# Attention and feed-forward in one kernel: softmax's end of odd batches in the left-over pass, three banks there, and three smaller moves

## The chip, the cores and the metric

The kernel runs on one core of a Trainium2 chip. The metric is device time in microseconds (us) of one execution, the median of several. The engines spoken of are TensorE (PE in the profile; its weight loads are a row of their own, PEld), VectorE (DVE), ScalarE (ACT) and the queue that starts transfers (SP). They run side by side; each works through its own list of instructions in order, and an instruction waits until what it reads is written and what it overwrites has been read.

## What is computed

Per batch (8) and head (8) the 576 positions are pooled into 32 slots and attended to; then a feed-forward layer with SiLU over all 4608 tokens (512 wide, 2048 inside). The reference, cut:

```python
a = np.exp(phi - np.max(phi, axis=2, keepdims=True))          # phi: batch, head, position, slot
a = a / (np.sum(a, axis=2, keepdims=True) + 1e-09)
k_m = np.einsum('bhsm,bhsd->bhmd', a, k)
v_m = np.einsum('bhsm,bhsd->bhmd', a, v)
scores = scale * np.matmul(q, k_m.transpose(0, 1, 3, 2))
scores = np.exp(scores - np.max(scores, axis=-1, keepdims=True))
attn = scores / (np.sum(scores, axis=-1, keepdims=True) + 1e-09)
x = np.matmul(attn, v_m)                                      # -> tokens x 512
h = x @ w_in
out = (h * (1.0 / (1.0 + np.exp(-h)))) @ w_out
```

## The kernel before

Everything is in 32 bits; a product of two such matrices is made of three matmuls, of high and low parts (hi*hi, hi*lo, lo*hi), so each operand exists as a rounded high part and the remainder, the low part. ScalarE usually makes the high part by a copy, VectorE the low part by a subtraction.

The kernel runs over the eight batches, b = 0 to 7. The attention of batch b+1 is computed in the gaps of batch b's feed-forward. v_m and w_in are multiplied first into one matrix P of the batch (`p_mm`, L631, then `p_split`: ScalarE L647 and VectorE L649), in four blocks of 512 columns; h is then the softmax times P. All blocks go through one tile in PSUM, `bg`, so a block's matmuls wait until VectorE has split the block before.

From batch 2 on the feed-forward goes in 16 steps, called slots (`for s in range(NFC)`, L1210): two halves t of the tokens, eight pairs j of 128-column groups each. A slot issues the h matmuls (`ffn1s`, L822), then `forms` (ScalarE's SiLU L836 and L838 and high parts L840 and L850; VectorE's sums L841 to L845 and low parts L851 and L852, all in the buffer `gbuf` and its splits), then whatever `events` hold for this slot (`run`), then the output products of the slot before (`st_step`, L861). These products are a Strassen-like scheme: four sums in four PSUM banks (tag `acc`, four buffers, given out in turn), 21 matmuls per step, 14 with the high part of the activations (HIGH) and 7 with the low part (LOW). After the last step of a half, `st_out` empties the banks: ScalarE copies banks 0 and 1 (L892), VectorE adds from banks 2 and 3 (L899), and four stores follow.

512 of a batch's 576 tokens go this way. The 64 others wait in `gleft` and are done for two batches together, behind each odd batch, in the left-over pass: four steps (slots 16 to 19) of `left_split` (ScalarE L924, VectorE L925) and `left_st` (24 matmuls, also L861, tiles `lsum`), the last of which is issued in slot 0 of the next batch. In two banks it keeps three sums; after the last step ScalarE copies a part of bank 0 (L945), VectorE adds it to the others (L946, L947), and the rows go out (L950).

What an event does and when is a table, `steady` (L957) for batches 2 to 6 and a list for batches 0 and 1 (L1018): `ev(b, slot, function, batch, ...)`. The names that matter: `s_max`, `s_sub`, `s_exp`, `s_sum` (VectorE L438 to L440) and `s_norm` (L444) are the softmax of the next batch; `s_back` turns it back (two VectorE transposes L459, one ScalarE copy L460 that is the high part) and `s_low` makes the low part (L467). FIRST and SECOND are halves of the tokens. `phi_max` (L258 to L261), `phi_fold` (L286 to L304, over small transfers) and `phi_sub` (L312, L315) prepare the exponential of phi for the batch after that. `exp_slots` (L828) are slots in which ScalarE changes its table for an exponential.

PE's and, from batch 1, ACT's lists keep the order in which the code is written. VectorE's list is laid out by the scheduler, which `behind(...)` ties at some places to the instruction before. In batch 0 events in the slots 11 and later stand behind the last split of SiLU's result; batches 0 and 1 use plain accumulation (`ffn1` L671, `ffn2` L714, `silu` L696 and L698).

## Time and profile before

| | us |
|---|---|
| median of three runs | 692.52 (690.91 to 693.7) |
| the profiled execution | 690.7 |
| its span in the profile | 688.9 |
| VectorE busy | 516.0 (75%) |
| ScalarE busy | 367.1 (53%) |

The span runs from the first to the last instruction of the profiled execution; the 1.8 us beside it are start and end. Rows of the timeline read: start, duration, engine, line, operation, tile written <- tiles read, shape, count; in brackets how long the engine had stood idle just before, and which instruction ended the wait. Several equal instructions are one row. Matmuls overlap: the next begins before the one ahead of it has left the array, so the start of the next row tells more than a row's duration.

### The profile page before, as it was taken

The page shows a single profiled execution, that of the slowest core. Times are in us where ns is not written, and L with a number is a line of the kernel's source. Part 1 is how long each engine was busy: PE and PEld are TensorE (multiplying, and loading weights), DVE is VectorE, ACT ScalarE, POOL GpSimd, SP SyncE. Part 2 cuts the span into 40 slices and gives each one's busy share as a digit, 9 for nine tenths or more (in the row PEclk, how much of TensorE's full clock was granted, in tenths as well). Part 3 has the DMA queues.
Part 4 walks back from the last instruction along what each step waited for, and adds up shares of the span by engine and source line. Part 5 has one row for each costly group of instructions (what it writes and reads, how often), then busy time and mean ns, then how long its engine had stood idle before and what let it go on. Part 6 is the DMA issues. An engine that isn't in the chain of part 4 may idle for free.

```text
span 688.9 us, 14787 instructions
## 1 busy us (share of the span) xinstructions
PE 675.3 (98%) x5932; PEld 596.0 (87%) x5932; DVE 516.0 (75%) x1085; ACT 367.1 (53%) x676; POOL 0.7 (0%) x6
## 2 busy tenths in 40 slices
PE   8899999999999998999999999999999999999997
PEld 3578777787889997899898999899989999889996
DVE  4897899988938588868885588876885668867652
ACT  3878684543535555644645546564653636554441
POOL 0000000000000000000000000000000000000000
PEclk9999999999999999999999999999999999999999
DMA  9988975224360561254420444125430204300001
GB/s 342 352 335 276 326 282 206 90 78 161 104 206 1 175 222 62 78 189 146 139 92 17 165 127 167 69 86 181 153 124 31 79 1 154 110 30 17 31 1 47
DMA packets 37748, 93.93 MB, mean 136 GB/s; under 512 B 4656, under 2 KB 21168, under 8 KB 34096
## 3 DMA queue, kind: packets, MB, share of 16 engines
q1 hardware_dynamic: 36736, 90.22, 38.0%
q10 hardware_dynamic: 944, 2.77, 1.0%
q8 instruction: 47, 0.77, 0.5%
q14 instruction: 21, 0.17, 0.1%
HBM read 77.22 MB, written 15.73 MB: 135 GB/s over the span
## 4 chain that ended last, share of the span: by engine, by line
PE 76%; DVE 6%; ACT 3%; issue 1%; DMA 1%; SPq 0%; DVEq 0%; ACTq 0%
PE sum L861 33%; PE h L822 21%; PE acc L714 5%; PE lsum L861 5%; PE bg L631 3%; PE h L671 3%; PE accleft L714 2%; PE bg L335 1%; PE bg L382 1%; DVE pm L649 1%; DVE gparts L688 1%; DMA fm<-fm 1%; ACT pm L647 0%; DVE aT L459 0%; DVE wf L782 0%
## 5 line engine op out<-in xcount | busy, mean ns | idle before, releaser
L822 PE MATMUL h<-aparts,pm 128*128 128x288 f32 x1152 | 169.1, 296 | 0.0
L822 PEld LDWEIGHTS h<-aparts,pm 128*128 128x128 f32 x1152 | 157.0, 188 | 1.2 <-issue 0.7
L836 ACT ACTIVATE gbuf<-h 128x512 f32<-128x512 f32 x96 | 57.2, 596 | 127.4 <-PE h L822 125.5
L861 PE MATMUL sum<-wo_hi,aparts 128*128 128x256 f32 x384 | 104.2, 293 | 0.7 <-ACT aparts L850 0.7
L841 DVE TENSOR_TENSOR gbuf<-gbuf 128x256 f32<-128x256 f32 x96 | 40.5, 422 | 83.0 <-ACT gbuf L836 82.5
L861 PE MATMUL sum<-kept,aparts 128*128 128x256 f32 x576 | 100.2, 282 | 0.0
L861 PE MATMUL sum<-wo_lo,aparts 128*128 128x256 f32 x384 | 100.0, 282 | 0.0
L861 PEld LDWEIGHTS sum<-wo_hi,aparts 128*128 128x128 f32 x384 | 72.7, 189 | 20.3 <-ACT gleft L838 16.7
L850 ACT ACTIVATE aparts<-gbuf 128x512 fp32r<-128x512 f32 x86 | 54.4, 633 | 65.8 <-DVE gbuf L845 65.8
L714 PE MATMUL acc<-wo_hi,gparts 128*128 128x512 f32 x256 | 85.1, 397 | 0.1
L861 PEld LDWEIGHTS sum<-kept,aparts 128*128 128x128 f32 x576 | 82.5, 191 | 0.0
L852 DVE TENSOR_TENSOR gparts<-gbuf,aparts 128x512 fp32r<-128x512 f32 x86 | 59.4, 691 | 18.6 <-ACT aparts L850 18.6
L861 PEld LDWEIGHTS sum<-wo_lo,aparts 128*128 128x128 f32 x384 | 73.1, 190 | 0.0
L861 PE MATMUL sum<-wo_hi,gparts 128*128 128x256 f32 x384 | 72.7, 281 | 0.0
L861 PE MATMUL sum<-kept,gparts 128*128 128x256 f32 x288 | 65.5, 282 | 0.0
L714 PEld LDWEIGHTS acc<-wo_hi,gparts 128*128 128x128 f32 x256 | 47.5, 188 | 14.0 <-DVE t L804 1.7
L861 PEld LDWEIGHTS sum<-wo_hi,gparts 128*128 128x128 f32 x384 | 59.4, 190 | 0.0
L671 PEld LDWEIGHTS h<-aparts,pm 128*128 128x128 f32 x372 | 51.8, 188 | 7.3 <-issue 2.7
L671 PE MATMUL h<-aparts,pm 128*128 128x288 f32 x372 | 56.1, 299 | 0.8 <-ACT aparts L599 0.4
L840 ACT ACTIVATE aparts<-gbuf 128x384 fp32r<-128x384 f32 x96 | 50.4, 525 | 0.0
L714 PE MATMUL acc<-wo_lo,gparts 128*128 128x512 f32 x128 | 49.4, 393 | 0.4 <-DVE wo_lo L182 0.3
L861 PEld LDWEIGHTS sum<-kept,gparts 128*128 128x128 f32 x288 | 47.9, 190 | 0.0
(204 smaller groups left out, 987.8 us busy)
## 6 DMA issues: line engine op xcount, KB each, us to landing
win<-win_saved SPq DMA_DIRECT2D x24, 1024.0 KB, 4.9
kv<-in_kv SPq DMA_DIRECT2D x28, 516.0 KB, 4.8
q<-in_q SPq DMA_DIRECT2D x16, 576.0 KB, 5.1
raw<-in_w_in SPq DMA_DIRECT2D x14, 512.0 KB, 7.3
raw<-in_w_out SPq DMA_DIRECT2D x6, 1024.0 KB, 6.8
win_saved<-win SPq DMA_DIRECT2D x4, 1024.0 KB, 8.7
phi<-in_phi SPq DMA_DIRECT2D x7, 576.0 KB, 5.9
out<-oo SPq DMA_DIRECT2D x26, 128.0 KB, 1.8
```

Source lines behind the costliest of these rows:

```text
L335: nc.tensor.matmul(pt[p][M * r : M * (r + 1), :KVW], e[:, p, c, M * r : M * (r + 1)], kvt[c][:, p, r], start=c == 0, stop=False, skip_grou ...
L382: nc.tensor.matmul(to[M * r : M * (r + 1)], kvT[D * p : D * (p + 1), 0, r], at[b]["q", hf][D * p : D * (p + 1), r, f : f + n], start=True, ...
L631: nc.tensor.matmul(bg[M * r : M * (r + 1), p, :w].rearrange("p (k f) -> p k f", f=P), kvT[D * p : D * (p + 1), 1, r], src[D * p : D * (p + ...
L671: nc.tensor.matmul(h[:, hf, :HALF], wt[:, p, fs], a[:, p, hf * HALF : (hf + 1) * HALF], start=n[hf] == 0, stop=n[hf] == 5, skip_group_chec ...
L714: nc.tensor.matmul(acc[key], gt[:, cs], wt[:, fc], start=fc == 0 and n == 0, stop=fc == NFC - 1 and n == 2)
L822: nc.tensor.matmul(h[:, i, :HALF], wt[:, p, f : f + P], a[:, p], start=n == 0, stop=n == 5)
L836: nc.scalar.activation(gbuf[:, :MAIN].rearrange("p (i f) -> p i f", i=2), h[:, :, :w], AF.Silu)
L840: nc.scalar.activation(hi[:, :3], g[:, 1:4], AF.Copy)
L841: nc.vector.tensor_tensor(g[:, 4:6], g[:, :1].broadcast_to([P, 2, P]), g[:, 1:3], op=ALU.subtract)
L850: nc.scalar.activation(hi[:, 3:], g[:, 4:], AF.Copy)
L852: last_split.append(nc.vector.tensor_tensor(lo[:, 3:], g[:, 4:], hi[:, 3:], op=ALU.subtract))
L861: nc.tensor.matmul(sums[bank][:, place * Q : (place + 1) * Q], gt[:, k], wt, start=bank not in begun, stop=True, skip_group_check=True,)
```

## The change

Six edits, all in the order of work and in where it lands; nothing is computed differently.

- `s_back` of batches 4 and 6, first half, and its `s_low` move from slot 14 of the batch before to slot 19, the last of the left-over pass. Its landing place there is the first half of `gbuf`, not the tile `cva`.
- `s_back` of batch 1 runs in two halves: four transposes of 288 and two copies.
- In the last step of each half of a batch, `st_step` issues the two LOW products of bank 0 ahead of the HIGH products of bank 2.
- `left_st` uses three banks and goes through them one after the other within a step; in the last step the copy and the first add follow as soon as their bank is done, and each half of the columns is stored on its own.
- In batch 2 `s_sum` moves from slot 12 to slot 11, `s_norm` from 13 to 12, and the second block of P of batch 3 from slot 14 to 15.
- `phi_sub` for batches 5 and 7 moves from slot 17 to slot 1 of the next batch, where it stands for the other batches already; and in batch 0 `phi_max` stands behind the last split.

```diff
@@ -453,11 +453,16 @@
             set_parts(b)
         w = u[1] - u[0]
         tag = "cva" if b > 2 else ("x", "y")[b - 1]
-        aT = at[b]["aT"][u] = sb.tile([P, 2, w], F32, tag=tag, name=f"aT{b}", bufs=1)
-        c = slice(*u)
-        for p in range(2):
-            last_turn[:] = [nc.vector.transpose(aT[:, p], at[b]["sc"][:, p, c])]
-        nc.scalar.activation(at[b]["ahi"][:, :, c], aT, AF.Copy)
+        if b > 2 and b % 2 == 0 and u == FIRST:
+            aT = gbuf[:, : 2 * w].rearrange("p (g s) -> p g s", g=2)
+        else:
+            aT = sb.tile([P, 2, w], F32, tag=tag, name=f"aT{b}", bufs=1)
+        at[b]["aT"][u] = aT
+        for v in (FIRST, SECOND) if b == 1 else (u,):
+            c, to = slice(*v), slice(v[0] - u[0], v[1] - u[0])
+            for p in range(2):
+                last_turn[:] = [nc.vector.transpose(aT[:, p, to], at[b]["sc"][:, p, c])]
+            nc.scalar.activation(at[b]["ahi"][:, :, c], aT[:, :, to], AF.Copy)
 
     def s_low(b, u):
         ahi, alo = (at[b][k] for k in ("ahi", "alo"))
@@ -879,8 +884,11 @@
         todo = (
             (0, 0, 0, b11), (0, 1, 2, b21), (3, 0, 1, t4), (1, 0, 6, b22), (1, 1, 4, b12), (2, 0, 5, t2), (2, 1, 3, t3)
         )
-        for terms in (HIGH, LOW):
-            for bank, place, k, w in todo:
+        order = [(HIGH, todo), (LOW, todo)]
+        if j == NP - 1:
+            order = [(HIGH, todo[:5]), (LOW, todo[:2]), (HIGH, todo[5:]), (LOW, todo[2:])]
+        for terms, some in order:
+            for bank, place, k, w in some:
                 product(bank, place, part, k, w, terms)
         if j == NP - 1:
             st_out(b, t)
@@ -927,27 +935,28 @@
 
     def left_st(b, n, gs):
         if n == 0:
-            sums[:] = [ps.tile([P, DMODEL], F32, tag="acc", name=f"lsum{i}", bufs=NI) for i in range(2)]
+            sums[:] = [ps.tile([P, DMODEL], F32, tag="acc", name=f"lsum{i}", bufs=NI) for i in range(3)]
             begun.clear()
         part = [x.rearrange("p (n f) -> p n f", f=P) for x in gs]
-        for i in range(2):
-            j = 2 * n + i
-            for k in range(2):
-                ws = [
-                    (wo_hi[:, 2 * j + k, q * Q : (q + 1) * Q], wo_lo[:, 2 * j + k, q * Q : (q + 1) * Q])
-                    for q in range(2)
-                ]
-                product(k, 0, part, 2 * i + k, ws[0], HIGH + LOW)
-                product(0, 1, part, 2 * i + k, ws[1], HIGH + LOW)
-        if n == NLS - 1:
+        last = n == NLS - 1
+        if last:
             o = sb.tile([P, DMODEL], F32, tag="cva", name="ol", bufs=1)
             x = sb.tile([P, Q], F32, tag="cva1", name="xl", bufs=1)
-            nc.scalar.activation(x, sums[0][:, :Q], AF.Copy)
-            nc.vector.tensor_tensor(o[:, Q:], sums[0][:, Q:], x, op=ALU.add)
-            nc.vector.tensor_tensor(o[:, :Q], sums[1][:, :Q], x, op=ALU.add)
+        for bank, (ks, q) in enumerate((((0,), 0), ((1,), 0), ((0, 1), 1))):
+            cs = slice(q * Q, (q + 1) * Q)
+            for i in range(2):
+                for k in ks:
+                    fc = 2 * (2 * n + i) + k
+                    product(bank, 0, part, 2 * i + k, (wo_hi[:, fc, cs], wo_lo[:, fc, cs]), HIGH + LOW)
+            if not last:
+                continue
+            if bank == 0:
+                nc.scalar.activation(x, sums[0][:, :Q], AF.Copy)
+                continue
+            nc.vector.tensor_tensor(o[:, cs], sums[bank][:, :Q], x, op=ALU.add)
             for k, r in enumerate((b - 1, b)):
-                q = nc.scalar if b == B - 1 and k else nc.sync
-                q.dma_start(out[r * S + MAIN : r * S + S], o[k * LEFT : (k + 1) * LEFT])
+                queue = nc.scalar if b == B - 1 and k else nc.sync
+                queue.dma_start(out[r * S + MAIN : r * S + S, cs], o[k * LEFT : (k + 1) * LEFT, cs])
 
     events = {}
 
@@ -974,14 +983,15 @@
         ev(b, 9 if early else 10, s_max, n, ALL)
         ev(b, 10, s_sub, n, ALL)
         ev(b, 11, s_exp, n, ALL)
-        ev(b, 12, s_sum, n, ALL)
-        ev(b, 13, s_norm, n, FIRST)
-        ev(b, 14, s_back, n, FIRST)
-        ev(b, 14, s_low, n, FIRST)
+        ev(b, 12 if early else 11, s_sum, n, ALL)
+        ev(b, 13 if early else 12, s_norm, n, FIRST)
+        turn = NFC + 3 if b % 2 else 14
+        ev(b, turn, s_back, n, FIRST)
+        ev(b, turn, s_low, n, FIRST)
         for k in range(3):
             ev(b, 10 + 2 * k, win_load, n, k)
         for k in range(2):
-            ev(b, 13 + k, p_mm, n, k * JW, JW)
+            ev(b, 13 + k if early else 13 + 2 * k, p_mm, n, k * JW, JW)
         m = n + 1
         if m < B:
             ev(b, ex + 3, load_kv, m, range(2))
@@ -990,7 +1000,7 @@
             ev(b, 7 if early else 12, phi_max, m)
             for i in range(3):
                 ev(b, 11 + i if early else 13 + i, phi_fold, m, i, load)
-            ev(*((b, NFC + 1) if b % 2 else (b + 1, 1)), phi_sub, m)
+            ev(b + 1, 1, phi_sub, m)
 
     for b in range(B):
         n = b + 1
@@ -1227,13 +1237,17 @@
                     finish((2 * part, 2 * part + 1))
                 traced = nc.cur_bb.bb.instructions
                 n = len(traced)
+                late = set()
                 for fn, a in events.pop((b, fc + part / 2), []):
+                    m = len(nc.cur_bb.bb.instructions)
                     fn(*a)
+                    if fn is phi_max:
+                        late.update(i.name for i in list(nc.cur_bb.bb.instructions)[m:])
                 if b == 0:
                     for i in list(nc.cur_bb.bb.instructions)[n:]:
                         if i.engine == ACT:
                             behind(i, last_silu[-1])
-                        elif i.engine == DVE and fc > 10:
+                        elif i.engine == DVE and (fc > 10 or i.name in late):
                             behind(i, last_split[-1])
             if b:
                 finish(range(NI))
```

How this moves instructions, at three places.

VectorE at the end of batch 2, slots 12 and 13, before (sc is the softmax of batch 3, ssm its sums, mt and mx the maxima of phi of batch 4, gbuf and gparts the SiLU forms of a slot):

```order
L438 TENSOR_REDUCE ssm<-sc_2582 128x36
L258 TENSOR_TENSOR mt<-phi_2478 128x512
L439 TENSOR_SCALAR ssm<-ssm 128x36
L841 TENSOR_TENSOR gbuf<-gbuf 128x256
L440 RECIPROCAL ssm<-ssm 128x36
L259 TENSOR_TENSOR mx<-mt 128x256
L844 TENSOR_TENSOR gbuf<-gbuf 128x128
L261 TENSOR_TENSOR mx<-mx,phi_2478 64x128 x2
L845 TENSOR_TENSOR gbuf<-gbuf 128x128
L851 TENSOR_TENSOR gparts<-gbuf,aparts 128x384
L852 TENSOR_TENSOR gparts<-gbuf,aparts 128x512
L649 TENSOR_TENSOR pm<-bg,pm 128x1024
```

and now, from the end of slot 11 (L846 stands where L841 stood, L857 where L852 did):

```order
L853 TENSOR_TENSOR gparts<-gbuf,aparts 128x896
L438 TENSOR_REDUCE ssm<-sc_2585 128x36
L439 TENSOR_SCALAR ssm<-ssm 128x36
L440 RECIPROCAL ssm<-ssm 128x36
L846 TENSOR_TENSOR gbuf<-gbuf 128x256
L849 TENSOR_TENSOR gbuf<-gbuf 128x128
L850 TENSOR_TENSOR gbuf<-gbuf 128x128
L856 TENSOR_TENSOR gparts<-gbuf,aparts 128x384
L857 TENSOR_TENSOR gparts<-gbuf,aparts 128x512
L444 TENSOR_TENSOR sc_2585<-sc_2585,ssm 128x2x288
L258 TENSOR_TENSOR mt<-phi_2481 128x512
L846 TENSOR_TENSOR gbuf<-gbuf 128x256
```

The sums went ahead of slot 12's forms, and the normalising (L444), which stood behind L649, ahead of slot 13's. On ScalarE the conversion of P's blocks, slots 13 to 15, before (pm<-bg is a block of P, aT the transposed softmax):

```order
L647 ACTIVATE pm<-bg 128x1024
L836 ACTIVATE gbuf<-h 128x512
L838 ACTIVATE gleft<-h 128x2x32
L840 ACTIVATE aparts<-gbuf 128x384
L850 ACTIVATE aparts<-gbuf 128x512
L647 ACTIVATE pm<-bg 128x1024
L460 ACTIVATE aparts<-aT_2884 128x2x288
L836 ACTIVATE gbuf<-h 128x512
```

and now:

```order
L652 ACTIVATE pm<-bg 128x1024
L841 ACTIVATE gbuf<-h 128x512
L843 ACTIVATE gleft<-h 128x2x32
L845 ACTIVATE aparts<-gbuf 128x384
L855 ACTIVATE aparts<-gbuf 128x512
L465 ACTIVATE aparts<-aT_2875 128x2x288
L841 ACTIVATE gbuf<-h 128x512
L843 ACTIVATE gleft<-h 128x2x32
L845 ACTIVATE aparts<-gbuf 128x384
L855 ACTIVATE aparts<-gbuf 128x512
L652 ACTIVATE pm<-bg 128x1024
L841 ACTIVATE gbuf<-h 128x512
```

The second conversion went behind the copy of aT and the forms of slot 15.

VectorE at the end of batch 3, slot 15, before:

```order
L649 TENSOR_TENSOR pm<-bg,pm 128x1024
L459 STREAM_TRANSPOSE aT_3828<-sc_3416 128x288 x2
L467 TENSOR_TENSOR aparts<-aT_3828,aparts 128x2x288
L841 TENSOR_TENSOR gbuf<-gbuf 128x256
L844 TENSOR_TENSOR gbuf<-gbuf 128x128
L845 TENSOR_TENSOR gbuf<-gbuf 128x128
```

and further on in the left-over pass, before:

```order
L925 TENSOR_TENSOR gparts<-gleft,gparts 128x512
L899 TENSOR_TENSOR oo<-x,sum_3560 128x256
L312 TENSOR_TENSOR phi_3322<-phi_3322,am 128x512
L315 TENSOR_TENSOR phi_3322<-phi_3322,am 64x128
L312 TENSOR_TENSOR phi_3322<-phi_3322,am 128x512
L315 TENSOR_TENSOR phi_3322<-phi_3322,am 64x128
L899 TENSOR_TENSOR x<-x,oo 128x256 x2
L925 TENSOR_TENSOR gparts<-gleft,gparts 128x512
L899 TENSOR_TENSOR x<-x,oo 128x256
L925 TENSOR_TENSOR aparts<-gleft,aparts 128x512
```

and now, in the same pass, up to slot 0 of batch 4:

```order
L933 TENSOR_TENSOR gparts<-gleft,gparts 128x512
L907 TENSOR_TENSOR oo<-x,sum_3563 128x256
L907 TENSOR_TENSOR x<-x,oo 128x256 x3
L933 TENSOR_TENSOR gparts<-gleft,gparts 128x512
L933 TENSOR_TENSOR aparts<-gleft,aparts 128x512
L464 STREAM_TRANSPOSE gbuf<-sc_3419 128x288 x2
L472 TENSOR_TENSOR aparts<-gbuf,aparts 128x2x288
L846 TENSOR_TENSOR gbuf<-gbuf 128x256
```

The transposes and the low part (now into and out of gbuf) left the place ahead of slot 15's forms and stand behind the last left-over split; the four subtractions of phi (L312, L315) are gone from the pass.

TensorE, the last matmuls of the program (lsum tiles in the order of their numbers are banks 0 and 1), before:

```order
L861 MATMUL lsum_7679<-wo_hi,aparts 128x256 x2
L861 MATMUL lsum_7679<-wo_lo,aparts 128x256
L861 MATMUL lsum_7679<-wo_hi,aparts 128x256 x2
L861 MATMUL lsum_7679<-wo_lo,aparts 128x256
L861 MATMUL lsum_7679<-wo_hi,aparts 128x256
L861 MATMUL lsum_7680<-wo_hi,aparts 128x256
L861 MATMUL lsum_7680<-wo_lo,aparts 128x256
L861 MATMUL lsum_7680<-wo_hi,aparts 128x256
L861 MATMUL lsum_7679<-wo_hi,aparts 128x256
L861 MATMUL lsum_7679<-wo_lo,aparts 128x256
L861 MATMUL lsum_7679<-wo_hi,aparts 128x256
```

and now (7686 to 7688 are banks 0 to 2):

```order
L866 MATMUL lsum_7687<-wo_lo,aparts 128x256
L866 MATMUL lsum_7687<-wo_hi,aparts 128x256
L866 MATMUL lsum_7688<-wo_hi,aparts 128x256
L866 MATMUL lsum_7688<-wo_lo,aparts 128x256
L866 MATMUL lsum_7688<-wo_hi,aparts 128x256 x2
L866 MATMUL lsum_7688<-wo_lo,aparts 128x256
L866 MATMUL lsum_7688<-wo_hi,aparts 128x256 x2
L866 MATMUL lsum_7688<-wo_lo,aparts 128x256
L866 MATMUL lsum_7688<-wo_hi,aparts 128x256 x2
L866 MATMUL lsum_7688<-wo_lo,aparts 128x256
L866 MATMUL lsum_7688<-wo_hi,aparts 128x256
```

Where banks took turns, the last twelve matmuls now all go to the third bank, and banks 0 and 1 are done before.

## The prediction

> **What bounds the kernel now.** I read the page's totals first, then the busy time by stretches, then the list of who waited for whom, cut down to TensorE, and last the timeline around each of those waits.
>
> ```profile
> span 688.9 us, 14787 instructions
> PE 675.3 (98%) x5932; PEld 596.0 (87%) x5932; DVE 516.0 (75%) x1085; ACT 367.1 (53%) x676; POOL 0.7 (0%) x6
> ...
> 260.00:280.00 20.00, 18.09 (x166) 15.01 (x165) 17.71 (x40) 9.86 (x20) 0.00 (x0) 1.00 0.29 101
> ...
> 660.00:689.00 29.00, 23.95 (x196) 23.55 (x194) 11.81 (x28) 7.90 (x17) 0.00 (x0) 0.98 0.09 28
> ```
>
> TensorE is the bound: 98% busy, at a granted clock of 1.00 in the stretch 260 to 280. The change removes no matmul, so it can only win what TensorE stands still: 1.9 us in that stretch, some 5 us around the end, and small gaps elsewhere. The waits that the change can reach are these (columns: microseconds in total, times, longest):
>
> ```profile
> PE bg L631 <- DVE pm L649: 1.9, 1, 1.9
> ...
> PE sum L861 <- ACT aparts L850: 0.7, 2, 0.4
> ...
> PE acc L714 <- DVE wo_lo L182: 0.3, 1, 0.3
> ...
> PE h L671 <- ACT gleft L698: 0.3, 1, 0.3
> ...
> PEld lsum L861 <- ACT oo L892: 0.9, 3, 0.3
> ```
>
> Together they hold 4.1 us, which with the tail is all there is to win: under 1% of 688.9. So the question is which of these waits goes and which comes back one step later. Batches are counted from 0 (b = 0 to 7).
>
> **Part C, the end of batch 2 (P's second block in slot 15).** This is the largest wait.
>
> ```profile
> 259.08 0.42 DVE L841 TENSOR_TENSOR gbuf<-gbuf 128x256 f32<-128x256 f32 x1 [2.00 <-ACT gbuf L836]
> ...
> 261.46 1.35 DVE L438 TENSOR_REDUCE ssm<-sc 128x36 f32<-128x1152 f32 x1
> ...
> 264.63 1.76 PE L822 MATMUL h<-aparts,pm 128*128 128x288 f32 x12
> ...
> 267.02 1.23 DVE L649 TENSOR_TENSOR pm<-bg,pm 128x1024 fp32r<-128x1024 f32 x1 [0.22 <-ACT pm L647]
> 268.16 0.75 DVE L444 TENSOR_TENSOR sc<-sc,ssm 128x576 f32<-128x576 f32 x1
> 268.30 1.09 PE L631 MATMUL bg<-win,kvT 64*32 64x512 f32 x16 [1.91 <-DVE pm L649]
> ...
> 273.18 0.83 DVE L459 STREAM_TRANSPOSE aT<-sc 128x288 f32<-128x288 f32 x2
> ...
> 274.04 0.69 ACT L460 ACTIVATE aparts<-aT 128x576 fp32r<-128x576 f32 x1 [2.04 <-DVE aT L459]
> ...
> 274.76 0.76 DVE L467 TENSOR_TENSOR aparts<-aT,aparts 128x576 fp32r<-128x576 f32 x1 [0.67 <-ACT aparts L460]
> ...
> 276.03 1.74 PE L822 MATMUL h<-aparts,pm 128*128 128x288 f32 x12
> 277.71 1.09 PE L631 MATMUL bg<-win,kvT 64*32 64x512 f32 x16
> ```
>
> Block 1 of P stands in slot 13 and block 2 in slot 14, and both use the one bg tile. Block 2 was due at about 266.3 (264.63 plus the 1.68 that lie between 276.03 and 277.71), but VectorE finished block 1's split (L649) only at 268.25. The change helps in two ways. The sum of exponentials (L438, 1.35, and two small ones) moves into the 2.00 us that VectorE idles ahead of 259.08, so it costs nothing there; and block 2 goes one slot later. But block 3 stays in slot 0 of batch 3, directly behind, so blocks 2 and 3 are now neighbours as 1 and 2 were. I carried the list of instructions on from 259.08 with these durations. VectorE: normalising (0.75, now in slot 12) and the rest as before let block 1's split start at about 266.1 instead of 267.02. Slot 14's group then runs from 268.1 to 270.6, the transposes (0.83) to 271.3, ScalarE's copy of them (0.69) to 272.1, the low part (0.76) to 272.8. Slot 15's SiLU stands behind that copy on ScalarE, its group on VectorE behind the low part: 272.8 to 275.2. ScalarE's conversion of block 2 ends at about 275.4, VectorE's split of it (1.23) at 276.6. TensorE without its wait is 2 us ahead of before: where before it was ready for block 3 at 277.71, it now is at about 275.6. So about 1.0 us of wait comes back in front of block 3, and 0.9 to 1.0 of the 1.9 is won. Bounds: 0 (the whole wait moves) and 1.9 (none does). **I take 1.0.**
>
> **Part D, the ends of batches 3, 5 and 7.** Batch 3's end:
>
> ```profile
> 351.63 0.40 PE L861 MATMUL sum<-kept,aparts 128*128 128x256 f32 x2
> 352.46 0.39 PE L861 MATMUL sum<-wo_hi,aparts 128*128 128x256 f32 x1 [0.43 <-ACT aparts L850]
> ...
> 353.95 1.09 ACT L892 ACTIVATE oo<-sum 128x512 f32<-128x512 f32 x2 [1.03 <-PE sum L861]
> ...
> 354.12 0.40 PE L861 MATMUL sum<-kept,gparts 128*128 128x256 f32 x2
> 354.61 0.39 PE L861 MATMUL lsum<-wo_hi,aparts 128*128 128x256 f32 x1
> 355.08 0.42 DVE L899 TENSOR_TENSOR x<-sum,x 128x256 f32<-128x256 f32 x1
> ...
> 360.12 0.69 DVE L925 TENSOR_TENSOR aparts<-gleft,aparts 128x512 fp32r<-128x512 f32 x1
> ...
> 363.34 1.74 PE L822 MATMUL h<-aparts,pm 128*128 128x288 f32 x12
> ```
>
> TensorE waits in slot 15's products for the late halves (0.43 here, 0.7 for batches 3 and 5), because transposes, copy and low part of batch 4's attention (the same chain as above, 273.18 to 275.52, so 2.34 us) stand ahead of slot 15's group. They move to slot 19. Then it waits for bank 0 (0.9 for three batches), which ScalarE copies from 353.95. Putting bank 0's two low products ahead of four of bank 2 lets that copy start four matmuls earlier; a matmul takes 0.12 (72 of them from 354.61 to 363.34), so 0.48, more than the 0.3 of one wait. Both go: 0.7 + 0.9 = 1.6, bounds 0 and 1.6. **I take 1.6.**
>
> What is late next: the moved chain must end before the next batch's first h (363.34). VectorE's last left-over split ends at 360.81, so 2.53 are left for 2.34. The max subtraction of the next batch but one, which stood among those splits, leaves too:
>
> ```profile
> 286.25 0.68 DVE L312 TENSOR_TENSOR phi<-phi,am 128x512 f32<-128x512 f32 x1
> ```
>
> Its two large operations alone give back 1.36, so the chain should be done 1.5 us ahead of h. In its new place, slot 1 of batches 4 and 6, this subtraction costs nothing if those slots behave as slot 1 of batch 3, where the row above already stands and TensorE shows no wait. The third bank is freed by the add at 355.08, done at 355.50; its first product comes twelve matmuls after the first of the pass, at 355.8: 0.3 us of cover.
>
> **Part E, the tail.**
>
> ```profile
> 683.77 0.28 PE L861 MATMUL lsum<-wo_hi,aparts 128*128 128x256 f32 x1
> ...
> 684.08 0.38 ACT L945 ACTIVATE xl<-lsum 128x256 f32<-128x256 f32 x1 [9.82 <-PE lsum L861]
> ...
> 684.50 0.42 DVE L946 TENSOR_TENSOR ol<-lsum,xl 128x256 f32<-128x256 f32 x1 [7.87 <-ACT xl L945]
> ...
> 685.28 0.47 SPq L950 DMA_DIRECT2D out<-ol  x1
> ```
>
> ```profile
> qz<-qm SPq DMA_DIRECT2D x16, 1.0 KB, 1.7
> ...
> out<-ol SPq DMA_DIRECT2D x5, 128.0 KB, 2.3
> ```
>
> From the last matmul's end (684.05) to the issue of the store are 1.23 us: a ScalarE copy and two adds. Now the copy and one add run beside bank 2's twelve products (1.4 us), and one add of 0.42 is left: 0.04 + 0.42 + 0.03 = 0.49, so 0.74 is won. The last store carries half the bytes on each queue: between nothing and 0.6 (128 KB landed in 2.3, 1 KB in 1.7); 64 KB is nearer to 128 KB, so 0.2. **I take 0.95, bounds 0.74 and 1.34.**
>
> The Trainium skill, "DMA: Bandwidth & Descriptors", section "Latency and other measured facts", says that the receipt from the target memory, not the bytes, makes up most of a DMA's fixed 2 us. By it the halved store would win almost nothing, and the sum below would be 0.2 smaller. The two rows above, 1.7 for 1 KB and 2.3 for 128 KB, lean towards the rule.
>
> **Parts A and B, batches 0 and 1.**
>
> ```profile
> 40.74 1.22 DVE L182 TENSOR_TENSOR wo_lo<-win,wo_hi 128x1024 fp32r<-128x1024 f32 x1
> ...
> 42.02 0.73 PE L714 MATMUL acc<-wo_lo,gparts 128*128 128x512 f32 x2 [0.33 <-DVE wo_lo L182]
> ...
> 105.36 1.17 ACT L460 ACTIVATE aparts<-aT 128x1152 fp32r<-128x1152 f32 x1 [3.29 <-DVE aT L459]
> ...
> 106.91 0.22 ACT L698 ACTIVATE gleft<-h 128x64 f32<-128x64 f32 x1
> ...
> 107.18 1.86 PE L671 MATMUL h<-aparts,pm 128*128 128x288 f32 x12 [0.33 <-ACT gleft L698]
> ```
>
> A: phi_max of batch 1 (its large operation is the 0.7 us kind) leaves VectorE's queue ahead of wo_lo's split, which so ends 0.6 earlier and no longer holds up TensorE: 0.33, bounds 0 and 0.4. **I take 0.3**, since ScalarE's order changes a little too. B: the SiLU that frees h stands behind the copy of the whole attention. In halves only 0.69 (the row at 274.04) stands ahead of it, and that half starts after two transposes of 288, not of 576. That is earlier by more than the 0.33, and the first h after it is 0.12 shorter (1.86 against 1.74). Two more transposes and one more copy cost 0.3 on engines that are not the bound here. **I take 0.45, bounds 0 and 0.45.**
>
> **Sum.** 1.0 + 1.6 + 0.95 + 0.3 + 0.45 = 4.3. The profiled execution took 690.7 (span 688.9); it would take 686.4 (span 684.6). It lies 1.8 under the median of the three runs, 692.52, so the median should come to 692.52 - 4.3 = 688.2.
>
> **Rivals.** (1) *Block 3 takes over the whole wait of block 2.* For it: both blocks share bg and are neighbours again, and VectorE is the busiest engine beside TensorE in that stretch (17.71 of 20). Against it: 1.35 us of VectorE's work goes into idle time. Price 1.0: 689.2. (2) *No wait comes back*, if slot 15's SiLU finds the copy done earlier than I reckon: 0.9 more won, 687.3. (3) *The third bank is not there in time, so the change to banks does not do what it says*: its cover is 0.3 us, and one split (0.69) ahead of the two adds that free it would turn this into a wait of 0.4 in each of three batches: 1.2 lost, 689.4. (4) *Slower*: the first h of batches 4 and 6 waits for the late attention. It decides from the point where VectorE's last left-over split ends less than 2.34 us before that h; then up to 2.34 stands bare twice, 4.7 lost against 4.3 won: 692.9. Against it speaks the 8.7 us left-over pass, in which VectorE now has less to do.
>
> **How the numbers follow.** Forecast 0.53, rival 1 0.20, rival 2 0.11, rival 3 0.11, rival 4 0.05. The range reaches over rivals 1 to 3 (687.3 to 689.4), widened by the spread of single runs (690.91 to 693.7, so 1.4 to either side): 685.9 to 690.9. A measurement of this kernel can tell about 0.5%, 3.5 us, from no change: faster means under 689.1. The forecast lies there in eight of ten, rival 2 nearly always, rivals 1 and 3 in about one of three: 0.42 + 0.11 + 0.10 + 0.04 = 0.67. Slower by that much needs more than rival 4 alone: 0.04. The rest, 0.29, is no change.
>
> **What would show it.** C: no wait before block 2, about 1 us before block 3, in the first slots of batch 3. D: no wait for L850 and none for bank 0 at the three ends; the moved copy on ScalarE done over 1 us ahead of the next h. E: about 0.5 us from the last matmul to the store's issue. A and B: the two 0.33 rows gone, and TensorE some 0.7 us earlier at batch 1's second slot. I am wrong if TensorE's waits add up as before, only with other names, or if loads from HBM, which no TensorE wait shows now, begin to appear in that list.

## The result, and the profile after

| | before | after |
|---|---|---|
| median, us | 692.42 (4 runs, 690.91 to 693.7) | 686.83 (4 runs, 685.86 to 687.41) |
| the profiled execution, us | 690.7 | 685.86 |
| its span, us | 688.9 | 684.0 |

The time after is 0.9919 of the time before (95% interval 0.9895 to 0.9943): faster, with the whole interval below 1. The medians fell by 5.6 us and the spans of the two profiled executions by 4.9, where 4.3 were forecast; since the forecast was added up from a profile, its terms are held against the spans. TensorE's granted clock is no part of the difference: it is 1.00 in each 100 us of both profiles up to 600, and 0.99 from there on. Lines of the new file stand up to 10 further down: P's matmuls are L636, its split L654, h L827, the output products L866, the copies of a finished bank L900, the last adds and stores L956 and L959.

The page's totals after, and the same two stretches as before the change:

```profile
span 684.0 us, 14812 instructions
PE 673.9 (99%) x5932; PEld 595.7 (87%) x5932; DVE 516.9 (76%) x1087; ACT 368.3 (54%) x677; POOL 0.7 (0%) x6
...
260.00:280.00 20.00, 19.12 (x175) 16.05 (x174) 17.28 (x38) 11.50 (x23) 0.00 (x0) 1.00 0.31 107
660.00:689.00 29.00, 20.46 (x170) 20.25 (x168) 10.12 (x23) 7.08 (x15) 0.00 (x0) 0.98 0.10 28
```

From 260 to 280 TensorE now stands still for 0.9 us, not 1.9. The list of TensorE's waits after (us in total, times, longest):

```profile
PE bg L636 <- DVE pm L654: 0.9, 1, 0.9
...
PE h L382 <- ACT gleft L843: 0.3, 1, 0.3
PE acc L719 <- DVE wo_lo L182: 0.2, 1, 0.2
PE h L827 <- ACT gleft L843: 0.2, 1, 0.2
```

The waits for the late halves and for bank 0 are gone. P's block still waits once, and there are three small waits which the list of before did not have in this form: for wo_lo (at 61 us instead of 42), and two for ScalarE's SiLU (at 243 us in batch 2's slot 9, and at 436 us where batch 5 starts; both are taken up below).

To see where each microsecond went, I set the two timelines beside each other at fixed places in the program. The start-up differs by some tenths from one execution to the next: the first h of batch 0 begins at 25.94 before, at 25.80 after, and between 25.73 and 26.41 in the experiments. So all starts in this table are counted from that h:

| start of | before | after | change on the way, us |
|---|---|---|---|
| batch 2's first h | 172.53 | 171.90 | -0.63 (A and B) |
| h of batch 2's slot 10 | 220.84 | 220.50 | +0.29 (not foreseen) |
| h of batch 3's slot 1 | 255.39 | 254.04 | -1.01 (C) |
| batch 4's first h | 337.40 | 334.93 | -1.12 (D) |
| h of batch 5's slot 2 | 422.49 | 420.24 | +0.22 (not foreseen) |
| batch 6's first h | 500.17 | 497.08 | -0.84 (D) |
| batch 7's first left-over product | 646.33 | 642.99 | -0.25 (D) |
| the last matmul | 657.83 | 654.38 | -0.11 (D) |
| end of the span | 662.96 | 658.20 | -1.31 (E) |

Together 4.76, and 0.14 of start-up. Now the places themselves. Part C, TensorE at the end of batch 2 and in batch 3's first slots:

```profile
264.15 1.76 PE L827 MATMUL h<-aparts,pm 128*128 128x288 f32 x12
...
268.25 1.76 PE L827 MATMUL h<-aparts,pm 128*128 128x288 f32 x12
269.94 1.09 PE L636 MATMUL bg<-win,kvT 64*32 64x512 f32 x16
...
273.58 1.74 PE L827 MATMUL h<-aparts,pm 128*128 128x288 f32 x12
276.20 1.09 PE L636 MATMUL bg<-win,kvT 64*32 64x512 f32 x16 [0.88 <-DVE pm L654]
```

The first row is the h of batch 2's slot 14. Block 2 (269.94) follows its h at once; block 3 (276.20) waits 0.88. Part D, the end of batch 3, TensorE's rows at the start of the left-over pass:

```profile
351.87 0.40 PE L866 MATMUL sum<-kept,gparts 128*128 128x256 f32 x2
352.11 0.28 PE L866 MATMUL lsum<-wo_hi,aparts 128*128 128x256 f32 x1
```

VectorE's rows there, the add that frees bank 2 and the moved attention:

```profile
352.83 0.42 DVE L907 TENSOR_TENSOR x<-sum,x 128x256 f32<-128x256 f32 x1
...
356.65 0.83 DVE L464 STREAM_TRANSPOSE gbuf<-sc 128x288 f32<-128x288 f32 x2
358.23 0.76 DVE L472 TENSOR_TENSOR aparts<-gbuf,aparts 128x576 fp32r<-128x576 f32 x1 [0.75 <-ACT aparts L465]
```

The left-over pass begins at 352.11, 0.24 after the two matmuls ahead of it, so without a wait. The moved attention is done at 358.99, and the h that reads it starts at 360.73: 1.74 us in hand. Bank 2 is free at 353.25, 0.3 ahead of the third tile's first product. Part E, the tail, in the timeline of all engines:

```profile
680.18 0.28 PE L866 MATMUL lsum<-wo_hi,aparts 128*128 128x256 f32 x1
680.50 0.42 DVE L956 TENSOR_TENSOR ol<-lsum,xl 128x256 f32<-128x256 f32 x1 [0.96 <-PE lsum L866]
```

And in the timeline of the queue that starts transfers, the last store's issue:

```profile
680.95 0.47 SPq L959 DMA_DIRECT2D out<-ol  x1
```

From the last matmul's end (680.46) to the last store's issue are 0.49 us. From that issue to the end of the span, with both ends taken from the trace to two places, are 683.99 - 680.95 = 3.04, and were 688.91 - 685.28 = 3.63 before.

### The profile page after: what moved, and what is told of

The parts are those of the page before. It is cut to its first block, busy times and chain, and to the rows that moved or that the text cites. A ratio compares the mean times of both kernels' runs of the same rounds, so it can differ in the third digit from the quotient of the medians.

```text
span 684.0 us, 14812 instructions
## 1 busy us (share of the span) xinstructions
PE 673.9 (99%) x5932; PEld 595.7 (87%) x5932; DVE 516.9 (76%) x1087; ACT 368.3 (54%) x677; POOL 0.7 (0%) x6
## 4 chain that ended last, share of the span: by engine, by line
PE 74%; DVE 7%; ACT 2%; issue 2%; DMA 1%; SPq 1%; DVEq 0%; ACTq 0%
PE sum L866 32%; PE h L827 20%; PE acc L719 6%; PE lsum L866 5%; PE bg L636 3%; PE h L676 3%; PE accleft L719 2%; PE bg L335 1%; DVE pm L654 1%; PE bg L382 1%; DMA fm<-fm 1%; DVE gbuf L846 1%; SPq L88 1%; ACT gbuf L841 1%; DMA qz<-qm 1%
## 5 line engine op out<-in xcount | busy, mean ns | idle before, releaser
L827 PE MATMUL h<-aparts,pm 128*128 128x288 f32 x1152 | 169.1, 296 | 0.2 <-ACT gleft L843 0.2
L827 PEld LDWEIGHTS h<-aparts,pm 128*128 128x128 f32 x1152 | 157.0, 188 | 1.5 <-issue 0.7
L841 ACT ACTIVATE gbuf<-h 128x512 f32<-128x512 f32 x96 | 57.3, 596 | 124.5 <-PE h L827 122.6
L866 PE MATMUL sum<-wo_hi,aparts 128*128 128x256 f32 x384 | 104.0, 293 | 0.0
L866 PE MATMUL sum<-kept,aparts 128*128 128x256 f32 x576 | 100.1, 282 | 0.0
L866 PE MATMUL sum<-wo_lo,aparts 128*128 128x256 f32 x384 | 100.1, 282 | 0.0
L846 DVE TENSOR_TENSOR gbuf<-gbuf 128x256 f32<-128x256 f32 x96 | 40.5, 422 | 78.6 <-ACT gbuf L841 77.9
L866 PEld LDWEIGHTS sum<-wo_hi,aparts 128*128 128x128 f32 x384 | 72.8, 190 | 19.2 <-ACT gleft L843 15.9
L866 PEld LDWEIGHTS sum<-kept,aparts 128*128 128x128 f32 x576 | 82.6, 191 | 0.0
L857 DVE TENSOR_TENSOR gparts<-gbuf,aparts 128x512 fp32r<-128x512 f32 x86 | 59.4, 690 | 18.5 <-ACT aparts L855 18.5
L866 PE MATMUL sum<-wo_hi,gparts 128*128 128x256 f32 x384 | 73.2, 281 | 0.0
L866 PEld LDWEIGHTS sum<-wo_lo,aparts 128*128 128x128 f32 x384 | 73.1, 190 | 0.0
L866 PE MATMUL sum<-kept,gparts 128*128 128x256 f32 x288 | 65.5, 282 | 0.0
L866 PEld LDWEIGHTS sum<-wo_hi,gparts 128*128 128x128 f32 x384 | 59.4, 190 | 0.0
L866 PEld LDWEIGHTS sum<-kept,gparts 128*128 128x128 f32 x288 | 47.9, 190 | 0.0
```

The source lines that it names most:

```text
L827: nc.tensor.matmul(h[:, i, :HALF], wt[:, p, f : f + P], a[:, p], start=n == 0, stop=n == 5)
L841: nc.scalar.activation(gbuf[:, :MAIN].rearrange("p (i f) -> p i f", i=2), h[:, :, :w], AF.Silu)
L846: nc.vector.tensor_tensor(g[:, 4:6], g[:, :1].broadcast_to([P, 2, P]), g[:, 1:3], op=ALU.subtract)
L857: last_split.append(nc.vector.tensor_tensor(lo[:, 3:], g[:, 4:], hi[:, 3:], op=ALU.subtract))
L866: nc.tensor.matmul(sums[bank][:, place * Q : (place + 1) * Q], gt[:, k], wt, start=bank not in begun, stop=True, skip_group_check=True,)
```

## The experiments

Twelve kernels, each the changed one with one edit unless said otherwise. The effects are tenths of a microsecond, below what a time can tell, so the readings come from the profiles, one of each kernel, with starts counted from batch 0's first h.

| kernel | median, us | of before (95%) | span | first h at |
|---|---|---|---|---|
| c_alone | 690.16 | 0.9985 (0.9976 to 0.9995) | 688.5 | 26.41 |
| sum_alone | 686.44 | 0.9930 (0.9915 to 0.9945) | 684.4 | 26.16 |
| slot_alone | 687.31 | 0.9947 (0.9930 to 0.9965) | 685.4 | 26.36 |
| third_late | 685.16 | 0.9912 (0.9897 to 0.9926) | 683.0 | 26.08 |
| one_store | 686.29 | 0.9922 (0.9899 to 0.9944) | 684.4 | 26.31 |
| turn14 | 687.42 | 0.9937 (0.9916 to 0.9957) | 684.8 | 25.73 |
| banks_old | 687.34 | 0.9936 (0.9914 to 0.9959) | 684.9 | 26.14 |
| max_first | 686.49 | 0.9923 (0.9905 to 0.9942) | 684.7 | 26.09 |
| whole_back | 686.21 | 0.9908 (0.9883 to 0.9933) | 684.6 | 26.24 |
| act_shift | 685.81 | 0.9903 (0.9882 to 0.9924) | 684.2 | 26.02 |
| late_shift | 685.14 | 0.9892 (0.9873 to 0.9911) | 683.2 | 25.93 |
| late_whole | 685.37 | 0.9896 (0.9877 to 0.9914) | 683.6 | 26.00 |

### Part C: the sum's move or the later slot?

**c_alone**, the kernel before with part C alone:

```diff
-        ev(b, 12, s_sum, n, ALL)
-        ev(b, 13, s_norm, n, FIRST)
+        ev(b, 12 if early else 11, s_sum, n, ALL)
+        ev(b, 13 if early else 12, s_norm, n, FIRST)
...
-            ev(b, 13 + k, p_mm, n, k * JW, JW)
+            ev(b, 13 + k if early else 13 + 2 * k, p_mm, n, k * JW, JW)
```

> The kernel before with part C alone (the sum of exponentials and the normalising one slot earlier, P's second block in slot 15, for batches 1 and 2). If C stands on its own as predicted: no wait in front of block 2, 0.9 us (0.7 to 1.1) in front of block 3, and a span 1.0 us under that of before, 687.9. If C's gain leaned on the other parts: a wait of 1.5 to 1.9 in front of one of the two blocks and a span of 688.5 to 688.9.

From slot 14's h to block 3 it takes 12.05 us, exactly as in the changed kernel (13.08 before), with the same 0.88 in front of block 3. C does not lean on the other parts. Of the span it won only 0.4, since its start-up took 0.47 longer; in the medians 0.9.

**sum_alone** and **slot_alone** take the two halves of C apart:

```diff
 sum_alone
-            ev(b, 13 + k if early else 13 + 2 * k, p_mm, n, k * JW, JW)
+            ev(b, 13 + k, p_mm, n, k * JW, JW)
 slot_alone
-        ev(b, 12 if early else 11, s_sum, n, ALL)
-        ev(b, 13 if early else 12, s_norm, n, FIRST)
+        ev(b, 12, s_sum, n, ALL)
+        ev(b, 13, s_norm, n, FIRST)
```

> The changed kernel with P's second block back in slot 14; the sum and the normalising stay early. Theory 1, the saving is VectorE's 0.9 us alone and the slot only decides where the rest of the wait is seen: block 2 waits 0.9 to 1.1 us, block 3 does not wait, span 684.0 within 0.2. Theory 2, the later slot saves time itself: both blocks wait, together over 1.4 us, span 684.5 to 685.0.

> The changed kernel with the sum and the normalising back in slots 12 and 13; P's second block stays in slot 15. Theory 1, the saving is VectorE's alone: the whole wait goes over to block 3 (1.7 to 2.0 us there, rival 1 of the prediction), span 684.9 to 685.1. Theory 2, the later slot saves time itself: block 3 waits 0.9 to 1.3, span 684.0 to 684.4.

TensorE's rows of sum_alone:

```profile
264.49 1.76 PE L827 MATMUL h<-aparts,pm 128*128 128x288 f32 x12
267.28 1.09 PE L636 MATMUL bg<-win,kvT 64*32 64x512 f32 x16 [1.03 <-DVE pm L654]
...
276.68 1.09 PE L636 MATMUL bg<-win,kvT 64*32 64x512 f32 x16
```

TensorE's rows of slot_alone:

```profile
264.74 1.76 PE L827 MATMUL h<-aparts,pm 128*128 128x288 f32 x12
...
270.53 1.09 PE L636 MATMUL bg<-win,kvT 64*32 64x512 f32 x16
...
274.17 1.75 PE L827 MATMUL h<-aparts,pm 128*128 128x288 f32 x12
278.19 1.09 PE L636 MATMUL bg<-win,kvT 64*32 64x512 f32 x16 [2.28 <-DVE pm L654]
```

With the sum early and block 2 in its old slot, block 2 waits 1.03, block 3 not at all, and the way to block 3 is 12.19: 0.89 of C's 1.03 is the sum's move. With the later slot alone the wait goes over to block 3 and grows to 2.28, more than either theory gave; the way is 13.45 (278.19 - 264.74), 0.37 longer than before the change. So the slot decides where the wait is seen, and is worth 0.14 only once the sum is out of the way. Taken in the other order, the slot costs 0.37 and the sum then wins 1.40; neither share is a constant of its edit. Theory 1 holds in the main. slot_alone is rival 1 of the prediction in pure form, and worse.

Why 2.28: in slot_alone VectorE starts block 2's split 12.17 after slot 14's h, in the changed kernel 10.77. That is 1.40 later, as much as the wait has grown: 0.92 of it is there already at block 1's split. The rest, 0.48, probably comes with the normalising (0.75), which stands behind that split again; no run separates the two.

**third_late**, block 3 of batch 3 one slot later:

```diff
-            ev(b, 0 if b > 2 else 1, p_mm, b, 2 * JW, JW)
+            ev(b, 0 if b > 3 else 1, p_mm, b, 2 * JW, JW)
```

> The changed kernel with P's third block of batch 3 in slot 1 in place of slot 0. If bg's split by VectorE is all that block 3 waits for: the wait of 0.9 us goes and none comes in front of block 4 in slot 2, span 683.1. Rival: blocks 3 and 4 are neighbours now, and 0.5 to 0.9 us comes back in front of block 4, span 683.6 to 684.0.

TensorE's rows of third_late in slots 1 and 2 of batch 3:

```profile
277.93 1.74 PE L827 MATMUL h<-aparts,pm 128*128 128x288 f32 x12
279.60 1.09 PE L636 MATMUL bg<-win,kvT 64*32 64x512 f32 x16
...
283.21 1.74 PE L827 MATMUL h<-aparts,pm 128*128 128x288 f32 x12
284.88 1.09 PE L636 MATMUL bg<-win,kvT 64*32 64x512 f32 x16
```

Blocks 3 and 4 follow their h by 1.67 each: no wait, and none for a split of P (L654) anywhere in its list. At batch 4's first h it is 0.75 ahead of the changed kernel; some 0.3 of the wait's price comes back as small delays, 0.23 of it in slot 3. The first theory holds, a little smaller than it said.

### Part D: the late attention and the order of banks

```diff
 turn14 (the tile of aT again in cva)
-        turn = NFC + 3 if b % 2 else 14
+        turn = 14
 banks_old
-        if j == NP - 1:
+        if False:
             order = [(HIGH, todo[:5]), (LOW, todo[:2]), (HIGH, todo[5:]), (LOW, todo[2:])]
```

> The changed kernel with the late attention of batches 4 and 6 back in slot 14 (its tile in cva again). If that move alone takes the waits for the late halves away: 0.4 us in front of a product at batch 3's end and 0.2 to 0.3 at batch 5's come back, none for bank 0, and TensorE starts the left-over pass of batch 3 0.4 to 0.6 later from batch 3's first h than in the changed kernel; span 684.7 (684.5 to 685.0), counted with the same start. Rival: with bank 0's low products brought forward the wait is hidden behind other products anyway, span 684.0.

> The changed kernel with the products of each half's last step in the old order. If the order is what frees bank 0 in time: 0.25 to 0.3 us in front of the first left-over product comes back at batches 3, 5 and 7, span 684.75 counted with the same start. Rival: the later adds also keep bank 2 from the third tile of the pass, 0.4 more at each, span 685.5 to 686.

The way on TensorE to the first left-over product, from batch 3's slot 1, from batch 5's slot 2, and to batch 7's from batch 5's:

| | before | after | turn14 | banks_old |
|---|---|---|---|---|
| batch 3 | 73.28 | 72.27 | 73.20 | 72.51 |
| batch 5 | 68.94 | 68.21 | 68.70 | 68.44 |
| batch 7 | 154.90 | 154.54 | 154.54 | 154.89 |

The attention's move is worth 0.93 + 0.49 = 1.42, the order of banks 0.24 + 0.23 + 0.35 = 0.82 up to the first products of the passes. Both theories hold, and neither rival: banks_old shows no third wait behind its 0.25 in front of the pass. TensorE's rows of banks_old there:

```profile
352.20 0.40 PE L866 MATMUL sum<-kept,gparts 128*128 128x256 f32 x2
352.69 0.39 PE L866 MATMUL lsum<-wo_hi,aparts 128*128 128x256 f32 x1
352.91 0.28 PE L866 MATMUL lsum<-wo_lo,aparts 128*128 128x256 f32 x1
```

After two matmuls of 0.12 the pass should start at 352.44; it starts 0.25 late, and its second product follows after 0.22, not 0.12. That second delay, 0.10, makes the pass itself 8.73 long in banks_old, as before the change, and 8.62 in the changed kernel. In batch 5 it is already in the 0.35 of the last row, in the passes of batches 3 and 7 it comes on top: the order of banks is worth 1.04 in all. Taken away singly, the two edits cost 2.46; the two together won 2.32 in the table of the result, because at batch 3 the waits partly cover each other.

What is new is the size of the attention's move. TensorE's rows of turn14:

```profile
349.22 0.40 PE L863 MATMUL sum<-kept,gparts 128*128 128x256 f32 x2
349.61 0.39 PE L863 MATMUL sum<-wo_hi,aparts 128*128 128x256 f32 x1
349.83 0.28 PE L863 MATMUL sum<-wo_lo,aparts 128*128 128x256 f32 x1
...
350.20 0.40 PE L863 MATMUL sum<-kept,aparts 128*128 128x256 f32 x2
351.02 0.39 PE L863 MATMUL sum<-wo_hi,aparts 128*128 128x256 f32 x1 [0.43 <-ACT aparts L852]
```

Two matmuls of 0.12 start at 350.20, and the next one at 351.02: it is 0.58 late where the wait says 0.43, and the one behind it follows after 0.22 (351.24), again 0.10 late. And the six matmuls from 349.22 on take 0.98 until 350.20; in the changed kernel the same six take 0.72. The third of them starts 0.15 late and the fourth another 0.10, without any entry among the waits. That adds up to the 0.93: 0.58 + 0.10 + 0.25. With batch 5 it is twice the 0.7 that the list of waits holds.

### Part E: does the last store's size matter?

**one_store** stores whole rows after the second add: as many bytes at the end as before the change, with its banks and adds as after it.

```diff
-                queue.dma_start(out[r * S + MAIN : r * S + S, cs], o[k * LEFT : (k + 1) * LEFT, cs])
+                if bank == 2:
+                    queue.dma_start(out[r * S + MAIN : r * S + S], o[k * LEFT : (k + 1) * LEFT])
```

> The changed kernel with whole rows stored after the second add, one store on each queue at the end (128 KB) in place of two of 64 KB; the adds and banks stay. From the issue of the last store to the end of the span lie 3.6 us before and 3.05 after the change. If the bytes of the last store make that difference: 3.6 us here, span 0.57 over that of the changed kernel. By the prediction's 0.2: 3.25. By the rule of the Trainium skill (DMA: Bandwidth & Descriptors, Latency and other measured facts) that the receipt and not the bytes makes up most of the fixed part: 3.05 to 3.1.

Its last matmul and store in the timeline:

```profile
680.05 0.28 PE L866 MATMUL lsum<-wo_hi,aparts 128*128 128x256 f32 x1
...
680.82 0.47 SPq L960 DMA_DIRECT2D out<-ol  x1
```

And its stores of the left-over rows in the list of transfers (KB each, median us from issue to landing):

```profile
out<-ol SPq DMA_DIRECT2D x5, 128.0 KB, 2.3
out<-ol ACTq DMA_DIRECT2D x1, 128.0 KB, 2.6
```

The span ends 684.44 - 680.82 = 3.62 after the issue, as before the change (3.63), against 3.04 with the halved stores. So the size of the last store makes the difference, 0.58; whether it is the bytes or the rows of 1 KB in place of 2 KB is not separated. The other kernels agree: 3.63 in c_alone, which also stores whole rows, and 3.04 to 3.07 in the ten others with halved stores. The span itself does not show the loss: counted from the first h it is 658.13, 0.06 less than in the changed kernel and not 0.57 more as expected, since 0.54 was won where batch 5 starts (last section).

### Parts A and B, and what B gave back

```diff
 max_first
-                        elif i.engine == DVE and (fc > 10 or i.name in late):
+                        elif i.engine == DVE and fc > 10:
 whole_back
-        for v in (FIRST, SECOND) if b == 1 else (u,):
+        for v in (u,):
             c, to = slice(*v), slice(v[0] - u[0], v[1] - u[0])
 act_shift (an event more in batch 1)
+            ev(b, 7, lambda: nc.scalar.activation(tiny[:, :1], ident[:, :1], AF.Copy))
```

> The changed kernel with batch 0's phi_max free again to stand ahead of wo_lo's split. If the tie is what removed the wait: 0.33 us in front of the wo_lo product at 42 us comes back; TensorE loses 0.2 to 0.35 by batch 1's start. Rival: the 0.18 us at 61 us, new with the change, is what it gave back, and it goes here, so that nothing is lost in the sum.

> The changed kernel with batch 1's attention turned back whole, as before. B's own gain by the forecast 0.45: the wait of 0.33 us for gleft at about 107 us comes back and TensorE reaches batch 2's first h 0.2 to 0.45 later. Second question: in the changed kernel ScalarE stands 0.17 us for nothing the profile shows ahead of the copies of a finished bank at 241.7 us, TensorE waits 0.26 behind it and loses 0.29 in batch 2's slot 9. Theory: this comes of ScalarE's list being one instruction longer, so here it goes, and the span is that of the changed kernel, 684.0 within 0.15. Rival: it comes of another part of the change and stays, span 684.2 to 684.5, counted with the same start.

> The changed kernel with one more ScalarE instruction, a copy of one column in batch 1 whose result nothing uses. Theory: the 0.17 us of ScalarE at 241.7 us belong to a place in its list, and one instruction more moves them ahead of another instruction, where ScalarE has time; TensorE's 0.26 us there go, span 683.7 counted with the same start. Rival: the stall belongs to the copies themselves, 0.17 stays, span 684.0.

Batch 2's first h is a sharp mark: it starts between 171.83 and 171.96 in the changed kernel and in all eight experiments that keep A and B. Without A it starts at 172.31 (the wait of 0.33 at 42 us is back, the 0.18 at 61 us is gone: a loss of 0.40 in all), without B at 172.36 (the wait of 0.34 for gleft is back: 0.45), without both at 172.53 (before) and 172.61 (c_alone). Taken away alone, A is worth 0.40, the upper bound of its forecast, and B its forecast; together they are worth 0.63 to 0.71, not 0.85.

B also has a price. ScalarE of the changed kernel in batch 2's slot 9 ("issue" is time in which the engine waited for nothing that the profile shows):

```profile
241.25 0.27 ACT L369 COPY kvT<-bg 128x128 f32<-128x128 f32 x1 [0.96 <-DVE kvT L368]
241.69 1.08 ACT L900 ACTIVATE oo<-sum 128x512 f32<-128x512 f32 x2 [0.17 <-issue]
```

TensorE of the changed kernel just behind it:

```profile
243.43 0.35 PE L382 MATMUL h<-q,kvT 64*32 64x64 f32 x16 [0.26 <-ACT gleft L843]
```

ScalarE of whole_back at the same place:

```profile
242.13 0.27 ACT L369 COPY kvT<-bg 128x128 f32<-128x128 f32 x1 [0.96 <-DVE kvT L368]
242.30 1.09 ACT L900 ACTIVATE oo<-sum 128x512 f32<-128x512 f32 x2
```

In the changed kernel the copies start 0.44 after the row ahead of them, in whole_back 0.17; the SiLU behind them is as late, and TensorE waits 0.26 for its buffer. Of 14 kernels the four with batch 1's attention whole (before, c_alone, whole_back, late_whole) do not show it. So it comes with B.

act_shift and late_shift, with yet one instruction more ahead, lose as much at the copies, and yet something has moved. In front of the copies stand two waits for semaphores (the signals by which engines and transfers tell that they are done), long fulfilled, which the timeline does not list. The view by line gives their first and last start. In the changed kernel:

```profile
L900 ACTq EVENT_SEMAPHORE  x2: 17/28/38, 241.3 to 241.3; - x2
```

In act_shift:

```profile
L900 ACTq EVENT_SEMAPHORE  x2: 17/28/38, 241.5 to 241.9; - x2
```

In the changed kernel, and in the seven others with its ScalarE list up to there, 0.36 to 0.38 pass between the second wait and the first copy; in act_shift and late_shift 0.33 pass between the two waits, and 0.08 to the copy. In the trace's list of ScalarE, waits included, that is in all ten the same place, ahead of the 320th entry. In the four others this place lies between the two copies, where ScalarE is busy anyway. So the stall belongs to the place in the list, as act_shift's theory had it; one instruction more moved it by one entry, still ahead of the copies, so nothing was won. Why ScalarE stops at that place stays open. B in sum: 0.45 won, 0.29 given back.

### Putting two gains together

**late_shift** is third_late with act_shift's instruction, **late_whole** is third_late with whole_back's edit.

> The changed kernel with P's third block of batch 3 in slot 1 and the one more ScalarE instruction in batch 1. Both gains add up if they are independent: span 682.7 counted with the same start, times 1.3 us under those of the changed kernel (ratio to before 0.990 to 0.991). Rival: only the block's move counts, span 683.0.

> The changed kernel with P's third block of batch 3 in slot 1 and batch 1's attention turned back whole. By theory the loss of 0.2 to 0.45 in batch 1 and the 0.29 won in batch 2 cancel: span 683.0 within 0.15 counted with the same start. Rival (the stall stays): 683.2 to 683.4.

Counted from the first h, their spans are 657.27 and 657.60, third_late's 656.92. Neither adds anything: act_shift won nothing to add, and B's two sides nearly cancel in late_whole. They lie 0.35 and 0.68 behind third_late, but batch 5's start alone makes 0.41 and 0.53 of difference (last section). The three medians (685.14, 685.37, 685.16) can't be told apart. The move of block 3 is what is left of it, some 0.75 us or 0.1% beyond the change; at that size the medians agree with it but don't prove it.

## Why the prediction was right, and where its terms were off

The forecast of 688.2 us (685.9 to 690.9) and the call of faster held, and the steps it named are the ones that happened. Point by point:

- **C, forecast 1.0, measured 1.01.** The step "about 1.0 us of wait comes back in front of block 3" is the row with 0.88. The reason given first, VectorE's sum going into idle time, carries 0.89 of it (sum_alone); the later slot, which I named beside it as a second help, 0.14. Rival 1 did not happen, and slot_alone shows on what that hung: with the sum in its old slot the whole wait goes over, and more.
- **D, forecast 1.6, measured 2.3 (1.12 + 0.84 + 0.25 + 0.11), above its bound.** The step that failed is "Both go: 0.7 + 0.9 = 1.6, bounds 0 and 1.6": it took the sum of the listed waits as the most that could be won. The banks were sized well: 1.04 for 0.9. The attention's move was mis-sized: 1.42 for 0.7, because a listed wait holds neither all of the delay in front of a matmul nor the 0.10 behind it, and one late start was not listed at all.
- **The moved chain, forecast "done 1.5 us ahead of h", measured 1.74.** Rivals 3 and 4 did not happen: no wait for the third bank (its cover is the 0.3 that I worked out), none for the late attention.
- **E, forecast 0.95, measured 1.31.** The path to the store came out as worked out, 0.49 us. The term for the halved store was 0.2 and is 0.58 in one_store and against before: near the upper bound of 0.6. The size was taken from two landing times, 2.3 for 128 KB and 1.7 for 1 KB. The 1 KB row is another kind of transfer (the same list of before has 3.8 for the 1 KB transfers of fm), and 64 KB is not nearer to 128 KB: in the trace the last stores land 0.35 sooner on the one queue (2.31 before, 1.96 after) and 0.42 on the other (2.63, 2.21), and the rest lies behind the landing. The Trainium skill's rule (DMA: Bandwidth & Descriptors, Latency and other measured facts), that the receipt (the target memory's answer that the data are there) makes up most of the fixed part, speaks of that part alone. The prediction and one_store's expectation read it as if a smaller store won nothing. That reading is refuted by the 0.58; the rule itself is neither borne out nor refuted here.
- **A 0.3 and B 0.45, measured 0.63 together**, with 0.29 given back in batch 2's slot 9, which nothing in the profile of before announced. B's extra copy was costed at nothing since ScalarE is not the bound; it put a stall of ScalarE where TensorE feels it.
- **phi_sub in slot 1 of batches 4 and 6, costed at nothing:** no wait shows in those slots. The 0.22 lost at batch 5's start is another thing (below).

The sum of 4.3 came near 4.9 partly by luck: D and E gave 1.1 more, A and B 0.1 less, B's price and batch 5's start took 0.5 back, and 0.14 is start-up, which no term named. Of the chances, 0.04 of the 0.67 for faster has no source among the terms named: those come to 0.63.

## What to carry to other kernels

A list of waits is no upper bound for what their removal wins: measure a wait by the starts of the matmuls around it, and add the stretches where they are merely spread. Where blocks share one buffer, moving one of them later wins only if the engine that frees the buffer has caught up by then: block 2 in slot 15 passed its wait on (slot_alone), block 3 in slot 1 lost it (third_late). Otherwise what wins is work taken off that engine, and the two edits should be tried apart. For a last store, time from its issue to the end of the span, not the median landing of all its like.

## What the runs showed of the hardware that was not expected

**A tiny transfer moves the whole by tenths.** In batch 4's slot 14 VectorE waits for a transfer of 1 KB (tile fm) in the middle of its list. VectorE's row in banks_old:

```profile
429.68 0.29 DVE L303 COPY wide<-fm 128x256 f32<-128x256 f32 x1
```

In the kernel before:

```profile
432.40 0.29 DVE L303 COPY wide<-fm 128x256 f32<-128x256 f32 x1 [0.80 <-DMA fm<-fm]
```

In max_first:

```profile
430.80 0.29 DVE L303 COPY wide<-fm 128x256 f32<-128x256 f32 x1 [1.15 <-DMA fm<-fm]
```

The way from batch 4's first h to batch 5's slot 2 is 84.77 to 84.79 us in the five kernels where that wait is 0 to 0.41 (third_late, banks_old, slot_alone, turn14, one_store), 85.09 at 0.80 (before), 85.19 at 0.91 (c_alone), 85.31 at 1.05 (after) and 85.42 at 1.15 (max_first); the five kernels not named fit in between. From about half a microsecond on, each tenth of that wait is a tenth of the kernel's time. The last of the three transfers of fm lands 3.25 to 3.45 us after its issue in the five and 4.15 to 4.40 in the nine others. The kernels do not differ in the code of that slot, so this is probably one source of the spread between executions; no kernel was profiled twice, so that is not shown. 0.22 of it fell on the changed kernel's profiled execution, against the one before.

**What a listed wait leaves out.** The list counts a wait from the end of the row ahead, but a matmul's row usually overlaps the next. A wait of 0.43 behind rows of 128x256 delayed the next matmul by 0.58 (turn14), one of 0.88 behind h by 0.95 (after against sum_alone), and one of 0.26 in batch 2's slot 9 by 0.27 (after against whole_back). What is added, 0.15, 0.07 and 0.01, is the usual overlap there: rows of 0.28 starting 0.12 apart, 0.29 against 0.22, and 0.35 against 0.34. A delay shorter than the overlap is not listed at all, like the 0.15 in turn14. And behind the stalls in front of a 128x256 product or of h the second matmul came 0.10 to 0.11 late: 0.22 after the first in place of 0.12 (turn14, banks_old), 0.24 in place of 0.13 (after, 436 us).
